# Four value buffers instead of two, a ring of four single mixer slices instead of three double ones, and a new order of the work

## The chip, the cores and the metric

The kernel runs on one NeuronCore of a Trainium2 chip. Five engines work side by side, each through its own queue in order: TensorE (PE in the profile, with PEld for its weight loads), VectorE (DVE), ScalarE (ACT), GpSimd (POOL) and SyncE (SP), which here does nothing but issue weight loads. Work on different engines is ordered by semaphores. The metric is the device time of one execution in microseconds. The kernel before takes 3266.26 us (median of three runs, 3263.81 to 3273.18).

## The reference

Four layers follow one another over a sequence of 2048 tokens of width 640: A, B, A, B, each of them as `x = x + layer(layernorm(x))`, with the same weights in both A and both B.

```python
# A: recurrent memory attention, 32 heads of 192, segments of 32 tokens, 8 memory rows
mem = mem0
for s in range(n_seg):                       # 64 segments, one after another
    h = concat([mem, x[segment s]])          # 40 rows
    q, k, v = h @ Wq, h @ Wk, h @ Wv
    p = softmax(where(mask, q k^T * scale, -1e9))
    o = (p v) @ Wo
    mem = o[:8]; outs.append(o[8:])
# B: shifted mixer with two MLPs
h  = gelu(layernorm(x) @ w1)                 # 640 x 640
hs = concat(four quarters of h, each shifted by 1 or 2 tokens) @ w2
x1 = x + hs
y  = x1 + gelu(layernorm(x1) @ w3) @ w4      # 640 x 1536, 1536 x 640
```

The memory makes the segments of one A layer strictly sequential: the queries of a segment need the output projection of the segment before.

## The kernel before

**Steps and lanes.** The two A layers run as two lanes, five segments apart (`LAG = 5`). A step `t` handles segment `t` of the first A layer and segment `t - 5` of the second one, together in one array of 80 rows (two times 32 tokens and 8 memory rows). There are 69 steps; the first five and the last five have one lane only. Between the lanes runs the mixer B, in chunks of 64 tokens of each lane: one chunk every two steps, 33 of them, and a last one after the attention has ended.

**A step.** `attention_step(t)` goes over the 32 heads in eight groups of four heads, which form four pairs. For a pair it loads three weight blocks (`load_pair`, kinds k, q and v): a part of them stays in SBUF for the whole run, the others are streamed in slices of 384 KB into a ring of 12 slots ("ra", tile `wst`). Then come keys and queries of the pair's first group (L928), the values of the whole pair (`values3` with L984 where both lanes run, `values` with L1024 otherwise), the attention of the first group, keys and queries of the second group and its attention. Attention (`attend`) is a chain: scores `pss` (PE L1044), mask and row maximum (DVE L1056), exponential (ACT L1063), sums and scaling (DVE L1067 to L1069), transposition `pst` (PE L1079), copy to `PT` (ACT L1087), product with the values `pso` (PE L1096), copy to `oT` (ACT L1104). `project` (L1122) multiplies with the output weights and adds up in `psy`; the projections of the last three groups stand at the end of the step. From `psy` the memory rows are copied to the next step's input `hT` (DVE L1149), which the next step's keys wait for.

**Values.** The product L984 uses TensorE in its 32-column mode: four small products side by side. An even step computes 96 rows (16 of them for the next step) in three PSUM banks, 60 matmuls for each pair; an odd step 64 rows in two banks, 40 matmuls. ScalarE copies the banks to the value tiles `V` (L964), four or six copies a pair; the rows that are handed from an even to an odd step go through `stash` (DVE L1007). The two value tiles, `Vt[0]` and `Vt[1]`, belong to the two groups of a pair, and are used again by the next pair. Besides that, an explicit order holds the values of a pair behind the last `pso` of the pair ahead:

```python
o_ = add("PE", mm_us(GWH, k=KC), s0 if r == 0 else s0 - STEP + 0.01 * r, fv, r=(*wbs, *src),
    w=tuple(banks) if r == 0 else (), a=(banks[r],) if r else (), mode=32,
    order=placed_before("pso") if r == 0 else ())
```

PSUM has eight banks: six for the attention ("A") and two for the mixer ("B").

**The mixer.** `chunk(c)` and `chunk_end(c)` add the attention's output to the residual, normalise, and run w1 (L1409), gelu, w2 (L1468), w3 (L1531), gelu and w4 (L1577). Its weights are streamed each time by `load_b` into a ring of three slots of two slices each ("rb", tile `wstB`, a slot of 2 x 640 columns): 19 loads for a chunk, 15 of 320 KB and 4 of 160 KB. One load feeds one piece of matmuls. At its end the chunk writes the next input rows of the second lane (`psn` L1631, ACT L1639). The last chunk uses the big ring and the freed resident weights instead.

**The order of the work.** The functions do not issue instructions; they add operations to a `Plan`, each with an engine, an assumed duration, its due time, and what it reads and writes. `Plan.place` then simulates the engines and places one operation after another: among the operations of an engine that could start within a short time of the first, it takes the one with the lowest rank, and on TensorE one in the mode that the array is in goes first. Ranks are numbers in a table `RANK` (one for each operation of a kind of step), found by a search; they may be any number of microseconds away from the due time. PSUM banks and ring slots are given out by the planner as well. The instructions are issued in that order, so each engine's queue is fixed when the kernel is built. Loads are issued by SP alone, in the order of their due times within each of the two rings, and each may be held until a certain matmul has ended ("pace"). The constant `OVER` says how long before the assumed end of an operation on ACT or DVE the next one of that engine may start in the planner's view.

**Small tiles.** `neghalf`, two `sm` (softmax maxima and sums) and five `st4` (layer norm statistics) are SBUF tiles of their own.

Of the kernel before, what the change touches and what calls it, by code (L numbers as in the profile page):

```python
# [24 lines left out]
RING_B = 3  # L25
# [18 lines left out]
VT_BUFS = 2  # L44
# [5 lines left out]
OVER = 0.0  # L50
# [18 lines left out]
        "apply_ln.f": (60.13, 185.694, 121.216, 72.37,),  # L69
        "chunk.f1": (175.755,),  # L70
        "chunk.f2": (76.908,),
        "chunk.f3": (157.464,),
        "chunk.fe": (133.631,),
        "chunk.fe3": (57.268,),
        "chunk.fel": (-12.647,),
        "chunk.fhr": (260.219,),
        "chunk.fhs": (203.515,),
        "chunk.fk0": (74.518,),
        "chunk.fk1": (194.333,),
        "chunk.fs": (103.426, 110.915,),  # L80
        "chunk.ft": (113.011,),
        "chunk.fw": (65.202, 75.684, 108.832, -50.712, 68.19, 10.815, 60.434, 122.265, 56.172, 161.413, 66.001,
            107.816, 153.37,),
        "chunk.fx": (114.535,),
        "chunk.fx0": (91.411, 111.515,),
        "chunk.fxu": (116.315,),
        "chunk.fz": (93.811,),
        "gelu.f1": (189.103, 112.842, 128.034, 132.117, 44.407, 147.123, 98.279,),
        "gelu.f2": (57.845, 81.849, 107.377, 125.496, 54.573, 170.821, 64.393,),
        "gelu.f3": (117.836, 38.035, 94.857, -4.703, 136.729, -25.232, 93.978,),  # L90
        "gelu.f4": (131.7, 41.437, 170.141, 69.53, 69.266, 116.495, 116.698,),
        "ln_ops.f1": (145.801, 200.678,),
        "ln_ops.f2": (71.886, 106.684,),
        "load_b.fn": (147.751, 23.09, 11.08, 11.355, 89.609, 6.762, 92.508, -1.573, 25.172, 111.488, 53.734,
            83.446, 82.888,),
        "transposes.f": (144.968, 58.96, 214.456,),
    },
    "chunk_end": {
        "apply_ln.f": (211.991,),
        "chunk_end.fc": (-27.709, 120.014, 238.626,),  # L100
        "chunk_end.fs": (74.033, 110.691,),
        "chunk_end.fst": (180.769, 113.382,),
        "chunk_end.ft4": (102.714,),
        "chunk_end.fw": (28.061, 167.286, 30.445, 89.214, 81.834, 168.442,),
        "chunk_loads.f": (195.767, 161.598, 81.116, 106.457, 112.814,),
        "chunk_loads.fz": (93.808,),
        "ln_ops.f1": (-34.553,),
# [1629 lines left out]
```

## Time and profile before

The profiled execution took 3268.68 us, of which the page's span is 3266.9 us; the other 1.8 us lie around it. It is 2.4 us above the median of the three runs.

| stretch | us | PE busy, as a share |
|---|---|---|
| first 100 us (weights that stay are loaded, one lane) | 100 | 61% |
| 100 to 300 us | 200 | 92% |
| 300 to 3000 us (two lanes) | 2700 | 97.7% to 99.6% in each 100 us |
| 3000 to 3200 us (one lane again) | 200 | 92% |
| the rest (last step, last chunk) | 67 | 78% |

Steps alternate: an odd step, with fewer values, is shorter. Between the copies of the memory rows (DVE L1149) lie on average 94.1 us for two steps; the shortest such two took 93.0 us, the longest 96.2 us.

Reading: "busy" of PE counts the pipelined tail of each matmul, so a share near 100% still has small gaps in it. They are seen in the timeline, where merged rows give the start of a run of matmuls, its length and their number: a matmul of 80 columns follows the one before after 0.036 us, one of 128 after 0.056 us, and four of the small value products take 0.163 us together. What starts later than that has waited.

### The profile page before, as it was taken

To read this page: it belongs to the slowest core of one execution; us is meant where nothing else is said; L and a number is where in the kernel's file an instruction comes from. 1 tells how busy PE (TensorE), PEld (TensorE's weight loads), DVE (VectorE), ACT (ScalarE), POOL (GpSimd) and SP (SyncE) were. 2 spreads that over 40 slices of the span, in tenths; PEclk is the share of its full clock that TensorE was granted. 3 is DMA by queue.
4 is the path that set the end of the run, shared out by engine and by line. 5 is a ranking of instruction groups with operands and counts; after the bars stand their busy time and mean duration, and the time that the engine had idled before them with its cause. 6 is when DMAs were issued, how large, how long until landed. Compare 5 with 4: busy or idle time off the path is not lost.

```text
span 3266.9 us, 172868 instructions
## 1 busy us (share of the span) xinstructions
PE 3149.0 (96%) x77161; PEld 2790.2 (85%) x77161; DVE 2285.5 (70%) x7377; ACT 1854.6 (57%) x4217; POOL 269.6 (8%) x510
## 2 busy tenths in 40 slices
PE   5899999999999999999999999999999999999997
PEld 4778888888888888888888888888888888888875
DVE  3566777777677777777777777777777777767665
ACT  2345565666556666656565666565656665556443
POOL 0000000000000000000000000000000000000000
PEclk8999999999999999999999999999999999999999
DMA  9787777778777877787777777777877787778885
GB/s 372 264 286 236 237 265 253 241 235 273 246 237 249 280 239 234 253 272 239 245 262 258 241 237 269 253 241 244 281 247 238 244 274 249 238 244 277 275 277 199
DMA packets 409714, 833.44 MB, mean 255 GB/s; under 512 B 39651, under 2 KB 207280, under 8 KB 408969
## 3 DMA queue, kind: packets, MB, share of 16 engines
q1 hardware_dynamic: 401704, 809.47, 73.2%
q0 software_dynamic: 7104, 12.84, 1.3%
q8 instruction: 604, 9.90, 1.2%
q14 instruction: 142, 1.16, 0.1%
q10 hardware_dynamic: 160, 0.08, 0.0%
HBM read 816.98 MB, written 5.24 MB: 252 GB/s over the span
## 4 chain that ended last, share of the span: by engine, by line
PE 88%; DMA 7%; issue 2%; DVE 2%; ACT 1%; SPq 0%; POOL 0%; POOLq 0%; ACTq 0%; DVEq 0%
PE psq L928 16%; PE psy L1122 16%; PE psk L928 16%; PE psv L984 15%; PE pss L1044 5%; PE pso L1096 5%; PE psh L1531 3%; DMA wst<-in_A_Wq_dram 3%; PE y L1577 3%; PE pst L1079 2%; DMA wst<-in_A_Wk_dram 2%; PE psv L1024 2%; PE psh L1409 1%; PE hs L1468 1%; DMA wst<-in_A_Wv_dram 1%
## 5 line engine op out<-in xcount | busy, mean ns | idle before, releaser
L928 PEld LDWEIGHTS <-wst 128*128 128x128 bf16 x19872 | 803.7, 99 | 64.1 <-issue 35.7
L1122 PE MATMUL psy<-oT,wo 128*128 128x80 bf16 (+1 forms) x16560 | 703.6, 200 | 26.4 <-issue 8.6
L964 ACT CAST V<-psv 96x384 bf16<-96x384 f32 (+3 forms) x1264 | 595.9, 474 | 168.3 <-PE psv L984 102.4
L1122 PEld LDWEIGHTS <-wo 128*128 128x128 bf16 x16560 | 630.8, 99 | 51.2 <-issue 35.1
L928 PE MATMUL psq<-hT,wst 128*128 128x80 bf16 (+1 forms) x9936 | 518.0, 200 | 13.7 <-DMA wst<-in_A_Wq_dram 8.6
L928 PE MATMUL psk<-hT,wst 128*128 128x80 bf16 (+1 forms) x9936 | 508.6, 200 | 17.7 <-DVE hT L1149 9.6
L939 ACT CAST qT<-psq 128x480 bf16<-128x480 f32 (+1 forms) x552 | 291.8, 529 | 371.2 <-PE psq L928 352.0
L1104 ACT CAST oT<-pso 128x480 bf16<-128x480 f32 (+1 forms) x552 | 293.7, 532 | 264.0 <-PE pso L1096 238.9
L954 DVE CAST kT<-psk 64x160 bf16<-64x160 f32 (+1 forms) x1104 | 340.4, 308 | 131.3 <-PE psk L928 62.6
L984 PEld LDWEIGHTS <-hT 128*32 128x32 bf16 (+1 forms) x11840 | 295.5, 96 | 157.0 <-issue 5.2
L1063 ACT ACTIVATE Pm<-pss,sm 80x320 bf16<-80x320 f32 (+2 forms) x552 | 279.3, 506 | 195.9 <-DVE sm L1056 105.2
L1056 DVE CUSTOM_DVE_ANT_1 pss<-pss,mask 80x320 f32<-80x320 f32 (+2 forms) x552 | 257.1, 466 | 150.1 <-PE pss L1044 138.3
L1087 ACT COPY PT<-pst 80x320 bf16<-80x320 bf16 (+2 forms) x552 | 221.7, 402 | 239.2 <-PE pst L1079 233.3
L984 PE MATMUL psv<-wst,hT 128*32 128x384 bf16 (+1 forms) x5920 | 343.3, 326 | 2.2 <-issue 1.1
L984 PE MATMUL psv<-wv,hT 128*32 128x384 bf16 x5920 | 344.7, 328 | 0.5 <-issue 0.5
L1067 DVE TENSOR_REDUCE sm<-Pm 80x4 f32<-80x320 bf16 (+2 forms) x552 | 250.5, 454 | 109.6 <-ACT Pm L1063 98.1
L928 PE MATMUL psq<-hT,wq 128*128 128x80 bf16 (+1 forms) x6624 | 321.1, 200 | 4.1 <-DMA wq<-in_A_Wq_dram 2.7
L928 PE MATMUL psk<-hT,wk 128*128 128x80 bf16 (+1 forms) x6624 | 321.0, 200 | 3.4 <-issue 2.0
L928 PEld LDWEIGHTS <-wk 128*128 128x128 bf16 x6624 | 270.8, 99 | 17.6 <-issue 13.9
L947 DVE CAST kT<-psk 128x320 bf16<-128x320 f32 (+1 forms) x552 | 253.8, 460 | 45.6 <-PE psk L928 33.5
L1069 DVE TENSOR_TENSOR Pm<-Pm,sm 80x320 bf16<-80x320 bf16 (+2 forms) x552 | 256.2, 464 | 34.9 <-DVE sm L1068 0.9
L928 PEld LDWEIGHTS <-wq 128*128 128x128 bf16 x6624 | 267.4, 99 | 6.5 <-DMA wq<-in_A_Wq_dram 3.0
(131 smaller groups left out, 3777.6 us busy)
## 6 DMA issues: line engine op xcount, KB each, us to landing
wst<-in_A_Wk_dram SPq DMA_DIRECT2D x556, 384.0 KB, 4.9
wst<-in_A_Wq_dram SPq DMA_DIRECT2D x556, 384.0 KB, 5.0
wst<-in_A_Wv_dram SPq DMA_DIRECT2D x418, 384.0 KB, 5.1
wstB<-in_B_w_dram SPq DMA_DIRECT2D x495, 320.0 KB, 4.7
wstB<-in_B_w_dram SPq DMA_DIRECT2D x132, 160.0 KB, 4.3
wo<-in_A_Wo_dram SPq DMA_DIRECT2D x8, 960.0 KB, 12.3
wv<-in_A_Wv_dram SPq DMA_DIRECT2D x2, 1536.0 KB
xw<-in_A_x_dram POOLq DMA_DIRECT2D x32, 77.5 KB, 5.3
```

The source lines that it names most:

```text
L928: nc.tensor.matmul(out=o[:, cc, 0:W], lhsT=wv(kc, GW * j + cc * P, GW * j + (cc + 1) * P), rhs=h[:, kc, cw:cw + W], start=begin(pq), stop= ...
L939: nc.scalar.copy(out=qT[:, :, c0:c0 + N], in_=T(pq)[:, :, off:off + N])
L947: nc.vector.tensor_copy(out=k4[:, :, 0::3, c0:c0 + N], in_=p4[:, :, 0::2, off:off + N])
L954: copy(out=k4[r0:r1, :, jj, c0:c0 + N], in_=p4[r0:r1, :, 1, off:off + N])
L964: (nc.vector.tensor_copy if e == "DVE" else nc.scalar.copy)(out=v_part(*dst), in_=a_)
L984: nc.tensor.matmul(out=o[32 * u:32 * u + n3, :], lhsT=left[:, kc, 32 * g3:32 * g3 + n3], rhs=wv(kc, a, a + GWH), start=(kc == 0), stop=(kc ...
L1056: nc.vector.tensor_tensor_reduce(out=o, in0=o, in1=maskt.unsqueeze(1).to_broadcast([NR, HG, N]), scale=-scale, scalar=3.0e38, op0=ALU.add, ...
L1063: nc.scalar.activation(out=Pb[0:NR, :, 0:N], in_=o, func=ACT.Exp, bias=sm_[0:NR, 0:1], scale=-1.0)
L1067: nc.vector.tensor_reduce(out=sm_[0:NR, 2:2 + HG], in_=Pb[0:NR, :, 0:N], axis=AX.X, op=ALU.add)
L1069: nc.vector.tensor_tensor(out=Pb[0:NR, :, 0:N], in0=Pb[0:NR, :, 0:N], in1=sm_[0:NR, 6:6 + HG].unsqueeze(2).to_broadcast([NR, HG, N]), op=A ...
L1104: nc.scalar.copy(out=o_[:, :, off:off + N], in_=T(pso)[:, :, 0:N])
L1122: nc.tensor.matmul(out=o[:, m, cw:cw + W], lhsT=wo[:, cc, m * P:(m + 1) * P], rhs=o_[:, cc, 0:W], start=st, stop=True, skip_group_check=True)
```

## The change

- **Value tiles**: four instead of two. A pair uses tiles 0 and 1 or 2 and 3, in turn (`vs[0] = i_ % 2`, `z = 2 * vs[0]`).
- **Order of the values**: the first and third pair of a step (`i_` 0 and 2) still come after the last `pso` placed. The second and fourth come after the values of the pair ahead (`end_v[-1:]`) and no longer after a `pso`. This holds in `values3`, that is where both lanes run. `values`, for one lane, keeps its order, but uses the four tiles too.
- **Mixer weights**: the ring "rb" has four slots of one slice (640 columns) instead of three of two slices. w1, w2 and w3's first ten column blocks are loaded and multiplied in single slices (`ONES`), w4 too; the last two column blocks of w3 (256 columns) come in three loads (`PAIRS`) instead of one. That makes 35 loads for a chunk: 32 of 160 KB, two of 128 KB, one of 64 KB, with 35 pieces of matmuls instead of 19. The bytes and the matmuls are the same. The last chunk keeps pairs.
- **Small tiles**: `neghalf`, `sm` and `st4` become columns of one tile `small` of 112 columns.
- **Planner**: `OVER` 0.03 instead of 0.0; all ranks in `RANK` are new, with more of them for the mixer's additional pieces.
- `v_copy` takes its destination when the operation is added, not when it is issued.

```diff
-RING_B = 3
+RING_B = 4
-VT_BUFS = 2
+VT_BUFS = 4
-OVER = 0.0
+OVER = 0.03
 RANK = {
     "chunk": {
-        "apply_ln.f": (60.13, 185.694, 121.216, 72.37,),
+        "apply_ln.f": (-7.128, 49.706, -1.253, 38.144,),
...
+    ONES = tuple((k, k + 1) for k in range(KC))
+    PAIRS = ((0, 2), (2, 4), (4, KC))
-    neghalf = ctile([P, 2], f32, "neghalf")
-    nc.vector.memset(neghalf[:], -0.5)
+    small = ctile([P, 112], f32, "small")
+    neghalf = small[:, 110:112]
+    nc.vector.memset(neghalf, -0.5)
-    sm = [ctile([P, 10], f32, f"sm{i}") for i in range(2)]
+    sm = [small[:, 90 + 10 * i:100 + 10 * i] for i in range(2)]
-    st4 = [ctile([P, 18], f32, f"st{i}") for i in range(5)]
+    st4 = [small[:, 18 * i:18 * i + 18] for i in range(5)]
-            b.make = lambda: wring.tile([P, SLOT if last else 2 * Dm], bf16, name="wst" if last else "wstB",
+            b.make = lambda: wring.tile([P, SLOT if last else Dm], bf16, name="wst" if last else "wstB",
+    end_v = []
-            return Vt[j][r0:r1, v0:v0 + 512].rearrange("n (a b) -> n a b", a=2)[:, :, 64 * hf:64 * hf + Dh]
+            return Vt[j + 2 * vs[0]][r0:r1, v0:v0 + 512].rearrange("n (a b) -> n a b", a=2)[:, :, 64 * hf:64 * hf + Dh]
         def values3(i_, pr, s0, wbs, wv):
+            vs[0] = i_ % 2
+            z = 2 * vs[0]
-                    order=placed_before("pso") if r == 0 else ())
+                    order=(placed_before("pso") if i_ % 2 == 0 else tuple(end_v[-1:])) if r == 0 else ())
                 if r == 0:
                     last_v.append(o_)
+                end_v.append(o_)
-                        v_copy(V_ODD[2 * r + hf], s0, banks[r], (64 * hf, 64 * hf + 64), (r, hf, 0, 64), B("V", r, hf, 0))
+                        v_copy(V_ODD[2 * r + hf], s0, banks[r], (64 * hf, 64 * hf + 64), (r, hf, 0, 64), B("V", z + r, hf, 0))
...
         def values(i_, pr, s0, wbs, wv):
+            vs[0] = i_ % 2
+            z = 2 * vs[0]
...
-            k_, V_ = kT[G % KT_BUFS], Vt[p_ % 2]
+            k_, V_ = kT[G % KT_BUFS], Vt[p_ % 4]
...
-        for i, (a, e) in enumerate(((0, 2), (2, 4), (4, KC))):
+        for i, (a, e) in enumerate(PAIRS if last else ONES):
-        for third, (n0, n1, units) in enumerate(((0, 5, ((0, 2), (2, 4), (4, KC))), (5, 10, ((0, 2), (2, 4), (4, KC))),
-                                                 (10, FC, ((0, KC),)))):
+        for third, (n0, n1, units) in enumerate(((0, 5, PAIRS if last else ONES), (5, 10, PAIRS if last else ONES),
+                                                 (10, FC, ((0, KC),) if last else PAIRS))):
-        for i in range(6):
-            a, e = 2 * i, 2 * i + 2
+        n4 = 2 if last else 1
+        for a in range(0, FC, n4):
+            e = a + n4
```

## The prediction

> **What bounds the kernel now.** I read the page first, for the bound and the chain.
>
> ```profile
> span 3266.9 us, 172868 instructions
> PE 3149.0 (96%) x77161; PEld 2790.2 (85%) x77161; DVE 2285.5 (70%) x7377; ACT 1854.6 (57%) x4217; POOL 269.6 (8%) x510
> ...
> PE   5899999999999999999999999999999999999997
> ...
> PE 88%; DMA 7%; issue 2%; DVE 2%; ACT 1%; SPq 0%; POOL 0%; POOLq 0%; ACTq 0%; DVEq 0%
> ...
> wstB<-in_B_w_dram SPq DMA_DIRECT2D x495, 320.0 KB, 4.7
> wstB<-in_B_w_dram SPq DMA_DIRECT2D x132, 160.0 KB, 4.3
> ```
>
> TensorE bounds it: it is busy in nine tenths or more of every slice but the first two and the last, and makes up 88% of the chain. The change leaves every matmul as it is, so only the holes between them can move. Next, the waits of TensorE between 300 and 3000 us, where both lanes run (engine and line, what it waited for: us in total, times, longest):
>
> ```profile
> PE psk L928 <- DVE hT L1149: 9.6, 29, 0.3
> PE psq L928 <- DMA wst<-in_A_Wq_dram: 5.4, 10, 1.1
> ...
> PE y L1577 <- DMA wstB<-in_B_w_dram: 1.0, 2, 0.6
> ...
> PE pso L1096 <- ACT PT L1087: 0.3, 1, 0.3
> ```
>
> No line says that TensorE waits for a value tile. The waits of the other engines, over the whole span, show the tiles themselves:
>
> ```profile
> DVE V L1007 <- PE pso L1096: 50.0, 71, 2.0
> ...
> ACT V L964 <- PE pso L1096: 6.1, 10, 1.3
> ```
>
> These are idle times of engines that are not the bound. So the wait that the change names costs TensorE nothing directly; what it costs is freedom of order, and that is to be looked for where the holes are. The timeline of TensorE at the end of an odd step (start us, length us, what, number of matmuls):
>
> ```profile
> 1520.57 0.97 PE L1122 MATMUL psy<-oT,wo 128*128 128x80 bf16 x15
> 1521.38 0.45 PE L1096 MATMUL pso<-PT,V 80*128 80x80 bf16 x8
> ...
> 1521.96 0.31 PE L1079 MATMUL pst<-ident,Pm 80*128 80x80 bf16 x4
> 1522.20 0.35 PE L984 MATMUL psv<-wv,hT 128*32 128x384 bf16 x4
> ...
> 1523.18 0.82 PE L984 MATMUL psv<-wst,hT 128*32 128x384 bf16 x16
> 1523.94 1.25 PE L1122 MATMUL psy<-oT,wo 128*128 128x80 bf16 x30
> ...
> 1525.85 0.31 PE L1079 MATMUL pst<-ident,Pm 80*128 80x80 bf16 x4
> 1526.12 0.70 PE L1122 MATMUL psy<-oT,wo 128*128 128x80 bf16 x15
> 1526.73 0.45 PE L1096 MATMUL pso<-PT,V 80*128 80x80 bf16 x8
> 1527.01 2.05 PE L1122 MATMUL psy<-oT,wo 128*128 128x80 bf16 x45
> 1529.39 0.81 PE L928 MATMUL psk<-hT,wst 128*128 128x80 bf16 x18 [0.33 <-DVE hT L1149]
> ```
>
> The reader is to see four things. The values of the last pair (1522.20) come right after a `pso` (1521.38), as the explicit order demands. Fifteen projections take 0.70 us where nothing holds them (1526.12), but 0.97 at 1520.57: a hole of 0.27. Forty-five should take 45 x 0.036 + 0.16 = 1.78, and take 2.05: again 0.27. From the fourth transposition at 1525.85 (four times 0.036, so done issuing at 1526.00) to 1526.12 there is 0.12. And the step's end, from the last projection (about 1528.86) to the first key (1529.39), costs 0.50 more than a matmul's spacing: the copy of the memory rows and its two semaphores.
>
> **The parts and their costs.** The sum is made against the profiled execution, 3268.7 us, which is 2.4 above the median of 3266.3.
>
> *1. Values of the second and fourth pair no longer behind a `pso`.* Where: the end of odd steps, of which 29 lie between 300 and 3000 us; even steps end without such holes, since the mixer's w3 fills them. Holes that an earlier last value group can close: 0.27 + 0.27 + 0.12 = 0.66 us, so 29 x 0.66 = 19 at most. They exist because the last pair's values and their four copies (ACT L964, 474 ns each by the page, 1.9 us) stand inside the last chain of attention; moved ahead, they leave ScalarE to `PT` and `oT`. The 0.50 at the very end stays: it is the hand-over of the memory rows, and no other work of TensorE is ready there. Bounds 0 to -19. I take two thirds, -13, as the projections that remain are cover for only a part of the last chain.
>
> *2. Two value groups side by side.* Entering and leaving the 32-column mode costs about 0.1 us each: sixteen small products from 1523.18 take 4 x 0.163 = 0.65, so the next could start at 1523.83 and starts at 1523.94. All of the 236 two-lane groups stand alone in this trace. The planner prefers work in the mode that the array is in, and may now join the second group to the first. An even step's two groups need 3 + 3 banks, all six of A; an odd step's 2 + 2. One join in each odd step saves 29 x 0.2 = 6; with both possible joins in every step 59 x 0.4 = 24, which banks and the ring of twelve (a fourth pair's k, q and v alone hold 4 + 4 + 4 slots) exclude. Bounds 0 to -12; I take -5.
>
> *3. Thirty-five loads for nineteen.* On SP: the sixteen more, at the shortest spacing of issues in this trace (0.475 us), add 7.6 us to a chunk's 94. SP's own longest waits are for pacing matmuls (558 us behind `psk` alone), so this is hidden; without that cover it would still lie on SP and not on TensorE, as the big ring holds work for about 25 us (an estimate: 1530 slices in 69 steps are 22 in a step of 47 us, and 12 slots). Behind a mixer load that waits for its slot stand SP's next loads for keys, queries and values. On TensorE: the pieces are finer, with the same matmuls. In depth: four slices are loaded ahead where it was six. A slot's round is a wait of its reader, 0.4 us issue and 4.3 us landing, some 5 us, so 1.25 us a slice. w1 (five slices in 3.5 us now, 1541.4 to 1544.9) and w2 (five in 3) would take about 2 us longer each; w3's 13 slices take 20 us and w4's 12 take 17 already, slower than the ring. That makes 4 us a chunk. The cover: the chunk's last copy to the next input (ACT L1639) ends at 1611.9, and the step at 1622.3: 10.4 us of slack. Bounds: 0, and one more wait of 0.54 a chunk (8.6 us in 16 waits of `psq` for `wst` over the span), 33 x 0.54 = +18. I take +3, near the present 1.0 us of `y`.
>
> [...] The rows speak for latency, not occupation: a half lands in 4.3 us and a whole in 4.7, while the big ring's loads are issued 1.1 us apart and land in 5.0.
>
> *4. One small tile, two more memsets.* Two more memsets of a `V` tile, 0.43 us each (0.91 for two now), before the first layer norm on DVE, which idles 0.49 there: +0.4 on a chain that later waits on DVE until 13.6 us anyhow, behind statistics of rows whose load lands at 12.4, with GpSimd's result ready at 8.0. A new order could lift that by up to 5.6 us, but the first 100 us move weights at a DMA share of 0.97. Bounds -5.6 to +0.9; I take -1.
>
> *5. One-lane steps and the last chunk.* There the order of the values is kept. Tiles that come free earlier give back part of 9 us of DVE and ACT idle time (2.8 and 6.1). Bounds -5 to +5 for their new order (the one-lane steps after the first took 38 to 44 us, so a new order may move each by a share of that); I take -1.
>
> *6. All the rest of the order.* Two steps took 93.0 to 96.2 us, mean 94.1, with the same work. If the new order made all like the shortest, 29 x -1.1 = -32; like the longest, 29 x 2.1 = +61. I take 0, as the mean is a fair sample of orders, and keep the ends for the range.
>
> Sum: -13 - 5 + 3 - 1 - 1 + 0 = -17, so 3252 against the profiled execution, and 3249 against the median. I say 3250. About 0.3% (10 us) is what a measurement of this kernel can tell from no change.
>
> **The rivals.**
>
> *Nothing moves (within 10 us).* TensorE has the same matmuls, and a new order fills some holes and opens others. For it: the named waits are not on TensorE's list. Against: 0.66 us in each odd step stands behind that order. Time: 3266 +/- 10.
>
> *Slower: value copies in front of the attention on ScalarE.* ScalarE takes its queue in order. Where a freed value group comes while the pair ahead attends, its four to six copies (1.9 to 2.8 us) stand between that pair's exponential, `PT` and `oT`. TensorE covers this as long as it has keys, queries or projections; near a step's end it has only three groups of projections, 3 x 30 x 0.036 = 3.2 us. For it: the waits for `oT` and `PT` are what opens the holes of part 1. Price: if one freed group in four is late by a copy row of 1.9, 59 x 2 / 4 x 1.9 = +56 before cover, perhaps half of that after: 3290. It decides from the point where more than one group in ten is late by a whole row (+22, more than the gain of 17).
>
> *Slower: the ring of four.* If the chunk becomes longer by more than its 10.4 us of slack, every second step waits for `xc` and its like: at 12 us, 33 x 1.6 = +53; my 4 us would have to be three times as long. Or SP stands behind a mixer load and the keys' weights come late; 33 x 0.54 = +18 as above. Time: 3285 to 3320.
>
> *Much slower: views of `small` are followed as one tile.* Then each maximum on DVE (L1056) would wait for the exponential that reads the other `sm`, 552 times 0.2 us or more: +110 at least. Against: GpSimd's copies to rows 96 to 99 of a `V` tile wait for `xw` and not for the engines that use the other rows, so parts of a tile are told apart.
>
> **How the numbers follow.** The forecast's case, 0.44; nothing moves, 0.22; ScalarE, 0.18; the ring, 0.12; one tile, 0.04. The forecast's own range is 3225 to 3256 (its parts at -36, of which 6 is order, and at the edge of what can be told). Range: the cases above 3300 hold about 0.12 (half of the ring's, a part of ScalarE's, the tile's), those below 3222 some 0.06. So 3222 to 3300. Faster 0.44, same 0.22, slower 0.34.
>
> **What the next profile would show.** Part 1: at the end of odd steps value groups that start before the `pso` of the pair ahead, runs of 15 projections at 0.70, and two steps nearer to 93.0. Part 2: runs of 80 small products. Part 3: `wstB` loads 1155 times, landing in about 4.3, waits of TensorE for `wstB` of a few us in all, and chunks that end before the step by less than 10.4 us. Part 4: DVE's first apply earlier than 13.6 or not. The prediction is wrong if TensorE's list names `PT`, `oT`, or `wstB` with tens of us, or if the two-step time rises above 94.1 with no name: then the order itself is worse.

## The result, and the profile after

The changed kernel takes 3275.7 us (median of 20 runs, 3266.6 to 3284.9) where the kernel before takes 3260.3 in the same series (20 runs, 3252.7 to 3273.2). The ratio is 1.0043, interval [1.0033, 1.0053]: slower by 0.43%, some 14 us, where the prediction said 17 us faster. The profiled spans are 3277.2 and 3266.9 us. So 10 us of the difference can be looked for in the two traces: the profiled execution of before lies 8 us above the median of its later series, and the other 4 us or so can't be placed.

The page of the kernel after, its busy times, the chain that ended last, and the mixer's loads (KB each, median us from issue to landing):

```profile
span 3277.2 us, 173629 instructions
...
PE 3146.0 (96%) x77161; PEld 2782.3 (85%) x77161; DVE 2280.3 (70%) x7379; ACT 1838.5 (56%) x4217; POOL 268.6 (8%) x510
...
PE 84%; DMA 12%; issue 2%; DVE 1%; ACT 1%; SPq 1%; POOL 0%; POOLq 0%; ACTq 0%; DVEq 0%
...
wstB<-in_B_w_dram SPq DMA_DIRECT2D x1056, 160.0 KB, 4.1
...
wstB<-in_B_w_dram SPq DMA_DIRECT2D x66, 128.0 KB, 4.3
```

Thirty-three more loads of 64 KB, in the trace's list of transfers, land in 4.4. TensorE still bounds the kernel, and its busy time has even fallen by 3 us. But the chain that sets the end now runs through transfers for 12% of the span, where it was 7%. The waits of TensorE between 300 and 3000 us say which transfers (us in total, times, longest):

```profile
PE psk L934 <- DMA wst<-in_A_Wk_dram: 8.0, 15, 1.3
PE psq L934 <- DMA wst<-in_A_Wq_dram: 8.0, 17, 1.3
PE psk L934 <- ACT hT L1655: 7.4, 29, 0.3
PE psk L934 <- issue: 2.6, 6, 0.8
PE psv L996 <- DMA wst<-in_A_Wv_dram: 1.5, 1, 1.5
...
PE psh L1546 <- DMA wstB<-in_B_w_dram: 0.8, 1, 0.8
PE hs L1483 <- DMA wstB<-in_B_w_dram: 0.8, 1, 0.8
PE y L1593 <- DMA wstB<-in_B_w_dram: 0.8, 1, 0.8
```

It is not the mixer's own weights in the ring of four that come late (2.4 us in all), but the keys' and queries' weights in the big ring: 16.0 us where it was 7.0. Over the whole span TensorE waits 32.3 us for weights; before it was 13.0.

What became of the step's end that the prediction read, in the kernel after (timeline of TensorE, the same odd step: start us, length us, what, number of matmuls):

```profile
1521.24 0.43 PE L1593 MATMUL y<-wstB,h2u 128*128 128x320 bf16 x2
1521.51 0.45 PE L1111 MATMUL pso<-PT,V 80*128 80x80 bf16 x8
1521.80 0.71 PE L1137 MATMUL psy<-oT,wo 128*128 128x80 bf16 x15
1522.34 0.31 PE L1094 MATMUL pst<-ident,Pm 80*128 80x80 bf16 x4
1522.58 0.35 PE L996 MATMUL psv<-wv,hT 128*32 128x384 bf16 x4
...
1524.32 0.99 PE L1593 MATMUL y<-wstB,h2u 128*128 128x320 bf16 x6
1525.15 0.45 PE L1111 MATMUL pso<-PT,V 80*128 80x80 bf16 x8
1525.43 0.31 PE L1094 MATMUL pst<-ident,Pm 80*128 80x80 bf16 x4
1525.58 1.78 PE L1137 MATMUL psy<-oT,wo 128*128 128x80 bf16 x45
1527.19 0.46 PE L1111 MATMUL pso<-PT,V 80*128 80x80 bf16 x8
1527.48 2.32 PE L1137 MATMUL psy<-oT,wo 128*128 128x80 bf16 x60
1529.63 0.32 PE L1647 MATMUL psn<-ident,h2u 128*128 128x64 bf16 x5
1530.20 0.98 PE L934 MATMUL psk<-hT,wst 128*128 128x80 bf16 x23 [0.26 <-ACT hT L1655]
```

Forty-five projections now take the 1.78 us that the prediction gave them without a hole. But the last pair's values (1522.58) still come behind a `pso` (1521.51). What fills the holes is the mixer's last product, `y`, which now stands between the projections; the chunk itself ends only with the step (`psn` at 1529.63), so its 10.4 us of slack are gone. The next step's keys now wait for the chunk's last copy (`hT` L1655, 29 times, 7.4 us) where they waited for the copy of the memory rows (29 times, 9.6 us).

To see where the time lies I took every distance between the starts of two matmuls, less the spacing at which matmuls of that width follow each other when nothing holds them (36 ns for 80 columns). What is left over is called a hole. Each hole was put down to late weights (the second matmul is the first reader of a load that landed less than 0.35 us before), to the instruction stream (a hole over 0.25 us that ends 1.15 to 1.65 us after a packet of the instruction queue has ended; more of that below), or to all else (waits for engines, the entry into the 32-column products and the way out, short holes). These are the sums between 302 and 2990 us for all kernels that were run, with the ratio of their time to before:

| kernel | ratio and interval | weights | instructions | all else | sum |
|---|---|---|---|---|---|
| before | 1 | 15.7 | 13.5 | 83.3 | 112.5 |
| after | 1.0043 [1.0033, 1.0053] | 31.5 | 11.3 | 71.4 | 114.2 |
| after_again | 1.0051 [1.0031, 1.0071] | 28.1 | 14.5 | 69.8 | 112.4 |
| after_e2 | 1.0224 [1.0201, 1.0246] | 10.3 | 63.9 | 75.3 | 149.5 |
| after_e2A | 1.0209 [1.0186, 1.0233] | 18.4 | 50.0 | 73.7 | 142.1 |
| after_e2B | 1.0009 [0.9997, 1.0021] | 24.7 | 12.7 | 68.6 | 106.0 |
| after_e4B | 1.0014 [1.0002, 1.0026] | 17.7 | 16.7 | 69.9 | 104.3 |
| after_ring6_e0 | 1.0045 [1.0024, 1.0065] | 23.7 | 11.4 | 70.1 | 105.2 |
| after_ring6_e4B | 1.0013 [0.9998, 1.0027] | 15.9 | 15.5 | 68.3 | 99.7 |
| after_sel | 1.0076 [1.0047, 1.0105] | 26.4 | 26.3 | 71.2 | 123.9 |
| after_x | 1.0068 [1.0045, 1.0090] | 29.2 | 13.7 | 68.7 | 111.6 |
| before_e2 | 1.0140 [1.0116, 1.0165] | 2.2 | 45.9 | 91.3 | 139.4 |
| before_e2B | 1.0087 [1.0072, 1.0102] | 9.0 | 32.1 | 88.8 | 129.9 |
| before_sel | 1.0051 [1.0034, 1.0069] | 4.9 | 20.6 | 87.2 | 112.7 |
| before_l1 | 1.0092 [1.0073, 1.0112] | 33.3 | 10.4 | 84.5 | 128.2 |
| before_split | 1.0114 [1.0093, 1.0135] | 31.1 | 21.7 | 81.4 | 134.2 |
| before_split2 | 1.0101 [1.0084, 1.0118] | 32.2 | 12.8 | 82.5 | 127.5 |
| before_half | 0.9945 [0.9927, 0.9963] | 4.3 | 4.9 | 81.9 | 91.1 |
| before_half_e2 | 0.9993 [0.9976, 1.0011] | 0.4 | 15.2 | 85.2 | 100.8 |

Read the column "all else" first: whatever is done to the loads, it is 81 to 91 us in the old order and 68 to 75 in the new. So the new order does give back 12 us (after against before) to 14 us (the means of the two orders) between the matmuls, near the 18 that the prediction's first two parts came to. The column "weights" takes it away again: 12 to 16 us more. Each profile is one execution, and single sums move by some 4 us from one to the next (after and its copy); drawing the limits between the classes a little differently moves single entries by up to 7 us. The profiled execution of after_again and of after_sel is the slowest of its series (13 and 14 us above the median), that of before_l1 the fastest (10 us below), and their rows are to be read so.

Most of the loss lies outside the two-lane steps. Measured by the ends of the steps, the profile after is 1.9 us behind at step 5, 4.5 at step 63, and 11.2 at step 67; the last chunk gives 0.9 back. In these last steps the holes for weights grew from 2.6 us to 10.2 (11.7 in the copy). The copy is 5.1 us behind at step 5, 4.8 at step 62 and 15.2 at step 67. So in the two-lane steps what the order gives and what the late weights take cancel; in the last one-lane steps the weights come late as well, and nothing is given back.

### The profile page after: what moved, and what is told of

The parts are those of the page before. It is cut to its first block, busy times and chain, and to the rows that moved or that the text cites. A ratio compares the mean times of both kernels' runs of the same rounds, so it can differ in the third digit from the quotient of the medians.

```text
span 3277.2 us, 173629 instructions
## 1 busy us (share of the span) xinstructions
PE 3146.0 (96%) x77161; PEld 2782.3 (85%) x77161; DVE 2280.3 (70%) x7379; ACT 1838.5 (56%) x4217; POOL 268.6 (8%) x510
## 4 chain that ended last, share of the span: by engine, by line
PE 84%; DMA 12%; issue 2%; DVE 1%; ACT 1%; SPq 1%; POOL 0%; POOLq 0%; ACTq 0%; DVEq 0%
PE psy L1137 16%; PE psk L934 16%; PE psq L934 16%; PE psv L996 14%; DMA wst<-in_A_Wq_dram 5%; DMA wst<-in_A_Wk_dram 4%; PE pso L1111 4%; PE pss L1059 4%; PE y L1593 3%; PE psh L1546 3%; PE pst L1094 2%; PE psv L1039 2%; PE psh L1424 1%; PE hs L1483 1%; DMA wstB<-in_B_w_dram 1%
## 5 line engine op out<-in xcount | busy, mean ns | idle before, releaser
L972 ACT CAST V<-psv 96x384 bf16<-96x384 f32 (+3 forms) x1264 | 585.2, 474 | 131.8 <-PE psv L996 61.3
L934 PE MATMUL psq<-hT,wst 128*128 128x80 bf16 (+1 forms) x9936 | 499.1, 200 | 18.0 <-DMA wst<-in_A_Wq_dram 13.7
L960 DVE CAST kT<-psk 64x160 bf16<-64x160 f32 (+1 forms) x1104 | 339.2, 307 | 81.4 <-PE pss L1059 53.3
L1082 DVE TENSOR_REDUCE small<-Pm 80x4 f32<-80x320 bf16 (+2 forms) x552 | 249.7, 452 | 181.2 <-ACT Pm L1078 179.0
L1078 ACT ACTIVATE Pm<-pss,small 80x320 bf16<-80x320 f32 (+2 forms) x552 | 278.4, 504 | 132.5 <-PE pst L1094 74.0
L1084 DVE TENSOR_TENSOR Pm<-Pm,small 80x320 bf16<-80x320 bf16 (+2 forms) x552 | 255.8, 463 | 40.7 <-PE pso L1111 0.5
L1102 ACT COPY PT<-pst 80x320 bf16<-80x320 bf16 (+2 forms) x552 | 222.1, 402 | 104.3 <-PE pst L1094 100.5
```

What stands on the lines that cost most here:

```text
L934: nc.tensor.matmul(out=o[:, cc, 0:W], lhsT=wv(kc, GW * j + cc * P, GW * j + (cc + 1) * P), rhs=h[:, kc, cw:cw + W], start=begin(pq), stop= ...
L960: copy(out=k4[r0:r1, :, jj, c0:c0 + N], in_=p4[r0:r1, :, 1, off:off + N])
L972: (nc.vector.tensor_copy if e == "DVE" else nc.scalar.copy)(out=part, in_=a_)
L1078: nc.scalar.activation(out=Pb[0:NR, :, 0:N], in_=o, func=ACT.Exp, bias=sm_[0:NR, 0:1], scale=-1.0)
L1082: nc.vector.tensor_reduce(out=sm_[0:NR, 2:2 + HG], in_=Pb[0:NR, :, 0:N], axis=AX.X, op=ALU.add)
L1084: nc.vector.tensor_tensor(out=Pb[0:NR, :, 0:N], in0=Pb[0:NR, :, 0:N], in1=sm_[0:NR, 6:6 + HG].unsqueeze(2).to_broadcast([NR, HG, N]), op=A ...
```

## The experiments

In all of them the order of the instructions is the one that the planner wrote, unless the text says otherwise; what is changed is when SP may issue a load. The code adds to each paced load a wait for the last matmul that the planner expects to be done by `PACE` (0.25 us) after the load's planned start.

### Does it recur?

after_again is the kernel after, unchanged.

> The changed kernel once more, for a second profile of it. Theory 'late weights' (the new order is as good, but the weights come too close to their use): again some 30 us of TensorE waits for streamed weights against 13 in the profile of before, spread over other places than in the first profile, and several short spells of half clock behind the longest of them; 0.3% to 0.6% slower than before. Rival 'order' (the new order itself has worse holes, and the waits for weights are an accident of one profile): the waits for weights fall to about 13 us and the kernel is as much slower all the same.

Measured: 3273.1 us, ratio 1.0051, waits for weights 29.2 us over the span (32.3). So the late weights belong to the kernel and not to one execution, though single places vary: of 53 late loads between 302 and 2990 us in the one profile and 55 in the other, 20 are the same.

What a late load looks like (kernel after, queue of SP: start, length of the issue, number of loads; then TensorE):

```profile
545.36 0.33 SPq L807 DMA_DIRECT2D wst<-in_A_Wq_dram  x1
546.50 0.33 SPq L845 DMA_DIRECT2D wstB<-in_B_w_dram  x1
547.06 0.33 SPq L807 DMA_DIRECT2D wst<-in_A_Wq_dram  x1
547.62 1.54 SPq L845 DMA_DIRECT2D wstB<-in_B_w_dram  x2
549.21 0.46 SPq L847 DMA_DIRECT2D wstB<-in_B_w_dram  x1
549.77 0.38 SPq L807 DMA_DIRECT2D wst<-in_A_Wv_dram  x1
550.54 1.26 SPq L807 DMA_DIRECT2D wst<-in_A_Wk_dram  x2
```

```profile
555.53 0.83 PE L996 MATMUL psv<-wv,hT 128*32 128x384 bf16 x16
557.87 0.35 PE L996 MATMUL psv<-wst,hT 128*32 128x384 bf16 x4 [1.50 <-DMA wst<-in_A_Wv_dram]
...
559.85 0.52 PE L934 MATMUL psk<-hT,wst 128*128 128x80 bf16 x6 [0.82 <-DMA wst<-in_A_Wk_dram]
560.16 0.73 PE L1111 MATMUL pso<-PT,V 80*128 80x80 bf16 x8
```

The values' slice, issued by 550.15, landed 7.7 us later, and the keys' slice 8.0. Counted like this from the end of the issue, the big ring's loads land in 4.6 us on average. Ahead of them stand six loads issued within five microseconds, four of them the mixer's. That holds in general: a late load of the big ring in the kernel after has on average 6.0 loads issued in the 5 us ahead of it, with 542 KB for the mixer (all loads of that ring: 4.4 and 268 KB), and lands in 5.9 us (4.6).

### All loads earlier

If weights come late by some tenths of a microsecond, releasing the loads earlier should mend it.

```diff
-PACE = 0.25
+PACE = -1.75
```

> The changed kernel in its own order on every engine; only the matmul that holds back a paced load is one that ends 2 us earlier, so the paced loads are issued up to 2 us earlier. Late weights: TensorE's waits for streamed weights fall from about 32 us to 15 or less, and the time by 8 to 18 us against the changed kernel, back to about the time of before (0.995 to 1.001 of before). Order: no change against the changed kernel, 1.003 to 1.006 of before. Ring of four slots as the bound: hardly a change, since loads held by a slot and not by the pace stay where they are.

> The kernel before with the same shift of its paced loads by 2 us. Late weights: there is less to take, 13 us of TensorE waits for weights in the profile, so 0 to 8 us faster. Order: no change. If more transfers at once disturb (instruction supply, other queues), slower by some us.

Measured: 3333.1 and 3304.3 us. The waits for weights fell as expected (over the span 32.3 to 9.3, and 13.0 to 4.2), but the time did not: both kernels became much slower. The time turned up in holes that no engine explains; TensorE's waits in after_e2 between 300 and 3000 us begin with

```profile
PE psy L1137 <- issue: 14.3, 25, 1.7
PE psq L934 <- issue: 13.5, 17, 1.8
PE psk L934 <- issue: 9.6, 14, 1.3
```

"issue" is time in which the engine waited for nothing that the profile shows. The next experiment split the edit: the big ring alone (after_e2A) and the mixer's ring alone (after_e2B, below).

```diff
-            while k >= 0 and done[k].end + PE_LAT > o.start + PACE:
+            while k >= 0 and done[k].end + PE_LAT > o.start + (PACE - 2.0 if o.slots and o.slots[0].cls == "ra" else PACE):
```

> The kernel after with only the loads of the big ring released up to 2 us earlier: the other half of after_e2, which cost 59 us. If the two halves act as after_e2 and after_e2B say, it is all here: 3310 or more, waits for weights 20 or less, holes without a name 50 or more. If only both together crowd the queues: below 3290.

Measured: 3324.9 us, and 50 us of holes put down to instructions. The loss of after_e2 is that of the big ring's loads.

### What the nameless holes are

The page of after lists a DMA queue of the kind "instruction", with the same figures in every kernel that was run:

```profile
q8 instruction: 604, 9.90, 1.2%
```

In the trace of after each of the 604 packets has 16384 bytes and they take 1.06 us on average. No view names the engine that they serve; that it is TensorE is an estimate from the counts: its 77161 matmuls and as many weight loads make 256 for each packet, and in the trace 255.8 of them start on average between the starts of two packets (164 to 340 in nine cases of ten). In before_e2 69 of the 121 holes over 0.25 us that are not for weights end 1.15 to 1.65 us after such a packet did, in before 23 of 76; that window is 9% of the span, so chance would give 11 and 7. All other holes of this kind hold 20.5 us in before and 20.4 in before_e2. So it looked as if data in flight kept TensorE's instructions waiting. To test it, half of the bytes of the mixer's two-slice loads were left out, with as many loads at the same times:

```diff
-            v = view()
+            v = view().v[:, 0:1, :] if not last and n == 2 else view()
+            e_ = a + 1 if not last and n == 2 else e
...
-                nc.sync.dma_start(out=v, in_=w1_v[:, a:e, :])
+                nc.sync.dma_start(out=v, in_=w1_v[:, a:e_, :])
```

> The kernel before with the first slice alone loaded of each two-slice mixer load (160 KB for 320, fifteen times a chunk), and read for both; as many loads at the same times, and the same matmuls. If holes of TensorE that follow instruction packets come from data loads that crowd the instruction stream: they fall from 13.5 us to below 9, waits for weights from 13 to below 9, time 3240 to 3256. If bytes don't matter there: holes 12 or more, time within 5 us of 3260.

> The same with all paced loads released up to 2 us earlier, as in before_e2 (3304 us, 46 us of holes behind instruction packets). If the data in flight make these holes: 30 us or less, and a time of 3265 to 3288. If it is the early release itself, whatever the bytes: 40 us or more and 3290 to 3305.

Measured: with 9% of all bytes left out, holes behind instruction packets fell from 13.5 to 4.9 us, and at the earlier release from 45.9 to 15.2; the other holes of the kind stayed at 20.6 and 20.3. The nameless waits of TensorE between 300 and 3000 us at the earlier release, first in before_e2, then in before_half_e2 (where L928 and L1122 are L937 and L1131):

```profile
PE psk L928 <- issue: 9.8, 16, 2.0
...
PE psq L928 <- issue: 7.3, 14, 1.3
PE psy L1122 <- issue: 6.1, 11, 1.3
```

```profile
PE psq L937 <- issue: 2.6, 7, 0.7
PE psk L937 <- issue: 1.8, 3, 0.7
PE psy L1131 <- issue: 1.5, 3, 0.8
```

The times are 3244.0 us, within what was expected, and 3258.5, below it. That these holes grow and shrink with the data in flight is shown by this; how the queues share the engines is not.

Most packets pass without such a hole: in before 23 holes stand behind the 508 packets between 302 and 2990 us (13.5 us in all); in before_e2 it is 69 holes and 45.9 us.

### The number of loads

before_split is the old order with each two-slice mixer load issued as single slices: 37 loads a chunk for 19, with ring and values as they were.

```diff
-                nc.sync.dma_start(out=v, in_=w1_v[:, a:e, :])
+            for i in range(n):
+                k, x = a + i, v[:, i:i + 1, :]
...
+                    nc.sync.dma_start(out=x, in_=w1_v[:, k:k + 1, :])
```

> The kernel before in its own order, with every mixer load of two or more slices issued as one load for each slice into the same slot: 37 loads for a chunk instead of 19, the same bytes. If the number of loads alone makes weights late (SyncE's issue time, more loads in flight at once), 5 to 20 us slower and more waits of TensorE for weights. If the number costs nothing and only the order and depth count: within 4 us of before.

Measured: 3295.9 us, slower by more than the 5 to 20 us expected. But this edit did more than one thing: the pacing wait stood on the last piece, and the first went out early. In before_split2 it stands on the first:

```diff
-                tc.add_manual_dep(o.last, done[k].last.name, dep, reason="pace")
+                tc.add_manual_dep(first, done[k].last.name, dep, reason="pace")
```

> The kernel before with its two-slice mixer loads issued as single slices, as in before_split, but with the pacing wait on the first piece of each (in before_split it stood on the last piece, so that the first pieces went out ahead of their time). If the number of loads is the price of part 3: again 3285 or more, waits for weights 25 or more. If before_split was slow because its first pieces were released early, as before_e2B is slow: below 3272, waits for weights below 20.

Measured: 3292.8 us, 33 more than before [27, 38], and the waits of TensorE between 300 and 3000 us (L928 is L930 here) begin with

```profile
PE psk L930 <- DMA wst<-in_A_Wk_dram: 10.6, 20, 1.6
PE psq L930 <- DMA wst<-in_A_Wq_dram: 10.1, 16, 1.5
```

Holes for weights doubled (15.7 to 32.2), all else stayed (83.3 and 82.5). So the number of loads has a price by itself, in an order that wasn't made for it: matched load for load, some of the keys' and queries' loads are issued later (the latest 2% by 0.9 us or more), and on average they land 5.0 us after the start of their issue instead of 4.9. The 594 loads more cost 33 us, or 0.06 us a load. Had each of them kept the queue occupied for the 4.3 us in which a load of 160 KB lands, that would make some 2550 us, an estimate from the page of before; so the time to landing does not occupy the queue, as the landings (160 KB in 4.3 us, 320 KB in 4.7) said before.

### Margins

In the kernel before the median load of the big ring is issued 7.85 us ahead of its first use and lands 3.5 us ahead; in after 6.9 and 2.5. Is the thinner margin enough to explain the loss? before_l1 makes the old order's margins thinner, by a release up to 1 us later:

```diff
-PACE = 0.25
+PACE = 1.25
```

> The kernel before, all paced loads released 1 us later, so that the median margin between landing and use falls from 3.5 us to the 2.5 us of the kernel after, with 19 loads a chunk as they are. Thin margins: TensorE's waits for weights rise from 13 to 30 to 65 us (275 loads of the old order are used less than 1 us after they land, and a sum over groups of these gives 51), holes behind instruction packets fall from 13.5 to below 10, and the time is 3275 to 3310. Number of loads: the old, few loads keep their cover, waits below 22 us and time within 8 us of 3260.

Measured: 3294.1 us; waits for weights over the span 28.4, just below the 30 expected, and holes behind instructions 10.4 for 13.5. Matched load for load, the big ring's loads went out only 0.4 us later on average. Thin margins alone, with the old number of loads, cost 30 us. The other way round, after_sel and before_sel release only the loads that the planner leaves under 0.3 us between landing and use, by 1 us, and the loads ahead of such a one no later than it:

```diff
+        use = min((x.start for x in o.succ if x.e == "PE"), default=1.0e9)
+        at = o.start + PACE
+        if use - o.land < 0.3:
+            at -= 1.0
+        early = min(early, at)
+        pace[o.i] = early
```

> The kernel after with its order untouched; only loads that the planner itself leaves under 0.3 us between landing and first use (about a quarter of the loads on SP) are released 1 us earlier, and those ahead of one of them in SP's order no later than it. Theory of thin margins (the new order issues its weights 6.9 us before use where the old one had 7.85, and that is the loss): TensorE's waits for weights fall from 29 to 32 us to 20 or less, the holes behind instruction packets grow by less than 10 us, and the time comes down by 5 to 15 us, to 3258 to 3270. Rival, number of loads (SP and the queue are busier with 35 loads than with 19, wherever they stand): the waits for weights stay at 25 or more and the time within 5 us of 3274. Rival, instruction supply (any load more in flight starves TensorE's instructions): the waits fall but the holes without a name grow by as much, and the time is 3275 or more.

> The same edit on the kernel before. Thin margins: little is to be had, as its waits for weights are 13 us in all: they fall to 5 to 9, the holes without a name rise by 3 to 8, and the time is within 8 us of 3260. Instruction supply: more than 10 us above.

Measured: 3287.2 and 3278.5 us, both worse than without the edit. In before the weights' holes fell to 4.9 us, those behind instructions rose to 20.6, and the time rose by 17. In after the weights' holes fell little (26.4), and those behind instructions rose from 11.3 to 26.3. My forecast by margins fell in both. In before it went as the rival "instruction supply" said. In after the waits for weights stayed (29.9 us over the span), as the rival "number of loads" had it, and the instructions came late besides; neither rival alone describes that. after_x moved the big ring's loads the other way, by up to 0.5 us, and the mixer's up to 2 us earlier:

> The kernel after, mixer loads released up to 2 us earlier as in after_e2B and the big ring's 0.5 us later. Of the two prices, instructions that come late and weights that come late, this lowers the first and raises the second: holes behind instruction packets below 10 us (12.7 in after_e2B), waits for weights 30 to 45 (26.6), time 3266 to 3285. Below 3262 would say that the big ring's loads were released too early.

Measured: 3279.9 us, with 31.0 us of waits for weights over the span, both within what was expected; the holes behind instructions, 13.7, are not lower. So for the big ring's loads both directions were tried, and both cost: with later ones TensorE waited 31.0 us for weights where after_e2B, below, has 26.6 (ratio 1.0068 for 1.0009), and with earlier ones, in after_e2A, the holes behind instructions were 50.0 us where after has 11.3 (1.0209 for 1.0043).

### The mixer's loads alone

after_e2B has the edit of after_e2A for the class "rb", the mixer's ring; after_e4B has 4 us for 2.

> The kernel after, only the mixer's loads (the ring of four) released up to 2 us earlier; as SP takes its queue in order, loads of the big ring ahead of them come earlier only where SP waited for a mixer load. If the ring of four is what is late (mixer loads at the head of SP's queue hold up the keys' and queries' weights): waits for weights fall from 30 to 15 or less and the time to 3255 to 3268. If a slot of the ring, not the release, holds the mixer loads: waits stay at 25 or more and the time within 6 us of 3274. If more loads in flight starve TensorE of instructions even so: the holes without a name rise by 15 or more and the time to 3285 or more.

> The kernel after with the mixer's loads released up to 4 us earlier. If the release held them: a little more than after_e2B gains, 3258 to 3266. If the four slots hold them by then (a slot is free only when the slice four ahead was read): as after_e2B, 3262 to 3270. If earlier loads crowd those of the big ring, as in after_e2: 3270 or more.

> The kernel before with only its mixer loads (19 a chunk) released up to 2 us earlier, as in after_e2B. If the late release of mixer loads is the price of the ring of four, whose load comes just ahead of its use and in a bunch with the big ring's loads, the old ring (two slices a load, six deep) has little to gain: within 5 us of 3260. If an earlier mixer load is worth as much in any order (about 8 us in after), the time is 3250 to 3255, and the gain has nothing to do with the change.

Measured: 3265.7 and 3265.2 us for after, 3288.9 for before. For before a time within 5 us of 3260, or a gain, had been expected. In after this is the one place where most of the loss can be got back: from 1.0043 and 1.0051 to 1.0009 and 1.0014. The waits for weights fell by less than I had asked for (26.6 and 20.2 us over the span; 15 or less was expected). Waits of TensorE in after_e2B between 300 and 3000 us:

```profile
PE psk L934 <- DMA wst<-in_A_Wk_dram: 8.1, 15, 0.9
...
PE psq L934 <- DMA wst<-in_A_Wq_dram: 5.5, 13, 1.0
...
PE psv L996 <- DMA wst<-in_A_Wv_dram: 1.4, 2, 0.9
...
PE psh L1546 <- DMA wstB<-in_B_w_dram: 0.3, 1, 0.3
```

In the old order the same edit is harmful, and in its list the nameless holes come next to the hand-over of the memory rows (9.6 us, as in before):

```profile
PE psk L928 <- issue: 8.6, 8, 2.4
PE psv L984 <- issue: 5.5, 5, 1.8
PE psy L1122 <- issue: 5.5, 9, 1.7
```

In after the mixer's loads moved by 0.24 us on average (matched load for load), in before by 0.61, with twice the bytes each.

Is it the four slots that hold them back? Two kernels have six slots, taken in turn (room was made by leaving out two of the last group's six slices of output weights):

```diff
+    turn = 0
+    for o in placed:
+        if o.dma and o.e == "SP" and o.slots and o.slots[0].cls == "rb":
+            o.slots[0].slot = turn % 6
+            turn += 1
```

> The same six slots with the release as in after. If slots that come free late hold up SP at the planned times (its queue stands, and the big ring's loads behind it): waits for weights fall from 30 to below 20, time 3258 to 3268. If only the release sets the time: as after, 3270 to 3278, waits 27 to 32.

> The kernel after, mixer loads released up to 4 us earlier, and six slots for four in the ring, taken in turn. For the room, the last group's output weights keep four of their six slices and two are used twice (320 KB less to load, once, at the start). If the four slots limit the loads (after_e4B gained no more than after_e2B, and issue to use was 6.76 us in both): issue to use rises above 7.5, waits for weights of TensorE fall below 20, time 3250 to 3262. If more mixer weights in flight crowd out the big ring's loads or the instructions: holes without a name 40 or more and time 3275 or more, as before_e2B.

Measured: 3273.2 us with the release of after, 3265.7 with the release 4 us earlier. The loads did move (by 0.78 and 1.22 us on average), and the waits for weights fell (24.6 and 16.9 us over the span), but the times are those of the kernels with four slots; for the second I had expected 3262 at most. So two slots more bring nothing that the times show, while an earlier release does; a gain of some 6 us lies within the interval of after_ring6_e0. Its one profile points two ways: between 302 and 2990 us the holes are as small as with the earlier release (105.2 us; 106.0 in after_e2B), but step 5 ends 5.5 us later than in after. Three kernels of the new order with the planned release have 1.0043, 1.0051 and 1.0045; three with mixer loads released earlier have 1.0009, 1.0014 and 1.0013. The difference of the means, 0.0034, is 11 us. In the profiles of the two sets the holes for weights between 302 and 2990 us are 27.8 and 19.4 on average (8.4 less), all holes there 110.6 and 103.3 (7.3 less), and all holes in the steps after 3030 us 53.2 and 49.8 (3.4 less): together about the 11.

What stays open: why earlier mixer loads help in the new order and cost 29 us in the old. More bytes a load and more movement go with it, and so do more holes behind instructions (32.1 for 13.5), but no run here changes one of these alone in the new order. Nor is it told apart whether the weights come late in the new order by the number of loads or by the thinner margins: in the old order each of the two alone raised the holes for weights by as much (15.7 to 32.2 and 33.3). And no run takes the change to pieces, so it is not shown whether the gain of the order needs the four value tiles. No kernel tried is faster than before with all its work done.

## Why the prediction was wrong

**What was right.** The bound, and that only holes between matmuls can move. That the value tiles' waits cost TensorE nothing directly. The place of part 1's holes, the ends of odd steps. The counts and landings of part 3 (1155 loads in 4.1 to 4.4 us, "about 4.3"), and that 2.4 us of TensorE's waits are for the mixer's weights ("a few us").

**Part 1: right place and size, wrong mechanism.** I gave -13 to value groups that come ahead of the `pso`. In the programs' order the second pair's values stand ahead of the last `pso` of the pair ahead in 30 of 59 steps, all of them even ones, and the last pair's in none. The holes at the end of odd steps closed because the mixer's products were put there: in the last 9 us of an odd step, hand-over included, "all else" is 1.20 us on average before and 0.59 after, and `y` and `psn` stand there in every one. The ends of even steps lost a little (0.28 to 0.41 us). That parts 1 and 2 came to -18 together and "all else" fell by 12 to 14 us is luck.

**Part 2: refuted.** I took -5 for value groups side by side. All 236 two-lane groups still stand alone (120 of 60 products, 116 of 40), and entering and leaving the 32-column products costs some 0.1 us each, as before: in both traces the first small product starts 0.13 us after the start of a projection (spacing 0.036), and the next matmul 0.26 us after the start of the last small product, where the next four small ones start after 0.15 (medians).

**Part 3 is the step that failed.** "I take +3", between 0 and +18, with the cover that "the big ring holds work for about 25 us". That estimate counted slots and not what is in them: loads are paced to matmuls, and the median load is issued 7 to 8 us ahead of its use, lands in 4.6, and has 2.5 to 3.5 us to spare. A bunch of six loads can use that up. In the old order the doubled number of loads cost 33 us. In the new order, which was made for it, the holes for weights grew by 12 to 16 us between 302 and 2990, and by 8 to 9 in the one-lane steps. Together that is 20 to 25 us where +3 stood, and above the bound of +18. (SP's own time was not what failed, though the shortest spacing of issues in the trace of before is 0.38 us and not 0.475.) The rival "the ring of four" had a branch for this, with its price: SP behind a mixer load, the keys' weights late, +18. I gave the whole rival 0.12. The trace of before had the row that should have raised it: `psq` already waited 5.4 us for `wst`, ten times. A wait for transfers said that the margin was already spent in some places, and more loads on the same queue met such places: in after `psq` waited 8.0 us, 17 times.

**Part 4: no gain.** I took -1 and a bound of +0.9; step 0 ended 1.5 us later (2.2 in the copy). Why is open.

**Part 5: wrong.** I took -1 for the one-lane steps and the last chunk; the one-lane steps at the end lost 6.8 and the last chunk gained 0.9, while the holes for weights grew by 7.6 there. This loss is the late weights of part 3 once more.

**Part 6: right as taken.** Two steps took 94.1 us on average and take 94.2. But the "0" stood for the order beside parts 1 to 3; it is the two-lane steps as a whole that stayed, because the order's gain and the late weights cancel.

**The other rivals.** ScalarE in front of the attention: between 300 and 3000 us TensorE's list has no wait for `oT` or `PT` in it; refuted there. One small tile: no sign of it; DVE is busy 2280 us (2286 before). "Nothing moves" was nearest in kind between 302 and 2990 us (112.5 and 114.2 us of holes), but not for the reason given.

## What to carry to other kernels

Depth of a ring in slots says nothing of the cover that a load has; count the time from its issue to its first use, and what it has left after landing (medians of 6.9 and 2.5 us in after). Here loads had an earliest time too: with all paced loads released up to 2 us earlier the holes behind instruction packets grew from 13.5 to 45.9 us in the old order and from 11.3 to 63.9 in the new, and the profile shows this only as waits without a name. A new order that closes holes by putting work closer together should be weighed with the waits for transfers that it makes, and the release of the few loads that stand ahead of the others is worth a trial of its own: it gave back 11 us in the new order here and cost 29 in the old.

## What the runs showed of the hardware

Each engine took its queue in order: in the trace of after the 77161 matmuls of TensorE, the 7379 operations of VectorE, those of ScalarE behind its first one and the 2728 loads of SyncE stand in the order in which the built program has them.

The queue q8, by its counts that of TensorE's instructions, moved 604 packets of 16384 bytes, of 1.06 us on average, in after. TensorE's holes behind its packets went with the data in flight: 4.9 us with the bytes of the mixer's two-slice loads halved (before_half), 13.5 in before, and 45.9 and 63.9 with all paced loads up to 2 us earlier (before_e2 and after_e2).

The granted clock fell to 0.50 for spells of 3.4 us. In after, apart from its start and end, this happened at 119.6, 559.9, 3072.2 and 3116.5 us; 0.9 to 2.1 us ahead of each a single distance between matmuls had ended, of 2.05, 1.83, 1.35 and 1.91 us. In the timeline above the `pso` at 560.16 takes 0.73 us, where the same eight products took 0.45 at 1521.51; gaps of 1.50 and 0.82 us with some 1.2 us of work between them stand ahead of that spell. Not every such gap was followed by one: between 100 us and the last 30 us of after, twelve distances of 1.3 to 1.6 us passed without a spell, and what tells them apart is not shown.
